# First channel product of batches 5 to 7 and of the tail chunk in seven products instead of eight, in a new searched order

## Chip, cores and metric

One core of one Trainium2 chip runs the kernel. The metric is the device time of one execution in microseconds (us). PE is the matrix engine (TensorE), PEld its weight loads, DVE is VectorE, ACT is ScalarE, POOL is GpSimd, SP is SyncE, which only issues transfers.

## What is computed

Random-feature attention over 8 batches, 8 heads, 576 positions and head size 64 with 128 features, then an MLP-mixer block on its output of width 512:

```python
def phi(x):                                   # x = q or k, scaled by 64 ** -0.25
    h = np.einsum('bhsd,md->bhsm', x, omega) - sum(x * x) / 2.0
    return np.exp(h - max(h)) / np.sqrt(m)
kv = np.einsum('bhsm,bhsd->bhmd', k_p, v)
num = np.einsum('bhsm,bhmd->bhsd', q_p, kv);  den = (q_p . sum over s of k_p) + 1e-06
x = num / den                                 # as [batch, 576, 512]
h = np.maximum(xt @ w_tok1, 0.0) @ w_tok2     # xt: [batch, 512, 576]; w_tok1 576x256
u = x + h.transpose(0, 2, 1)
h2 = np.maximum(u @ w_ch1, 0.0) @ w_ch2       # w_ch1 512x1536, w_ch2 1536x512
out = u + h2
```

## The kernel before

A batch has 512 main positions and 64 tail positions. The tails of all eight batches together make a ninth chunk of 512 positions, called the tail chunk, so the channel MLP runs over nine chunks of 512 positions. Matrix operands are fp16, accumulation is fp32 in eight PSUM banks.

For each batch, `attention` makes the features of k and q (PE, then an exp on ACT), a maximum per position (DVE, L680), its reciprocal (L682), the scaled v (`vs`, a two-input product in SBUF, mostly on POOL, recorded at L295 in the helper `tt`), the product kv (L701), and the numerators (L734, L736), which DVE divides (L743, L744) into the tile `x`. `token_mix` follows (L770, L777, L790), and its sum `u` (L793) is transposed by a DMA (L798) into `uT`.

`channel_mix` takes a chunk of `uT` (for the tail chunk `uTt`). The first channel product (L966) makes twelve blocks of 128 hidden channels; each is four matmuls of 512 columns into one bank, which one relu then moves to the tile `r3` (ACT at L290, or DVE at L292). From chunk 1 on, the second channel product (`channel_out_fast`, L916) already goes by Strassen's scheme in Winograd's form: seven products of 12 matmuls with 256 columns instead of eight, on sums of `r3` blocks that DVE makes in SBUF (tile `S`, L295, two halves of four sums of 128x768) and on weight sums `T` made once. DVE reads its banks to the tile `o` (L905), and SP and ACT store `o`.

All work is cut into jobs. A table of numbers, `ORDER`, sets the order in which the jobs are written out, `SLOT` which buffer or bank each takes, and `MOVED` which engine runs a job that may run on several. Each engine runs its own instructions strictly in that order and waits where an operand is not there. POOL's own queue also issues the loads of q, k and v; loads for later batches are cast to fp16 into DRAM and transposed from there by SP (L380).

Of the rings of buffers, `uT`, `qT`, `kT`, `x`, `u` and `r1` have three buffers each, `qp` and `kp` four, `r3` and `o` two.

Of the kernel before, what the change touches and what calls it, by code (L numbers as in the profile page):

```python
# [9 lines left out]
FP32 = mybir.dt.float32  # L10
# [158 lines left out]
def kernel(  # L169
# [12 lines left out]
    nc = tc.nc  # L182
# [888 lines left out]
```

## Time and profile before

| | |
|---|---|
| device time, median of 3 runs | 277.16 us (276.93 to 277.24) |
| span of the profiled execution | 275.9 us, that is 1.26 below that median; the profile lists no other time of its own for it |
| PE busy | 266.6 us (97%), 2503 matmuls |
| DVE busy | 222.9 us (81%) |
| ACT busy | 138.1 us (50%) |
| POOL busy | 91.2 us (33%) |
| granted PE clock | full in nearly all of the span |

The profile names an instruction by its line, engine and operation and by out<-in tiles. A group's row gives its busy time and the mean length of one instruction in ns; because instructions of one engine overlap a little in their pipeline, the distance from start to start is often shorter than that length. "Idle before" is how long the engine stood still ahead of such instructions, with what ended the wait.

### The profile page before, as it was taken

The page shows a single profiled execution, that of the slowest core. Times are in us where ns is not written, and L with a number is a line of the kernel's source. Part 1 is how long each engine was busy: PE and PEld are TensorE (multiplying, and loading weights), DVE is VectorE, ACT ScalarE, POOL GpSimd, SP SyncE. Part 2 cuts the span into 40 slices and gives each one's busy share as a digit, 9 for nine tenths or more (in the row PEclk, how much of TensorE's full clock was granted, in tenths as well). Part 3 has the DMA queues.
Part 4 walks back from the last instruction along what each step waited for, and adds up shares of the span by engine and source line. Part 5 has one row for each costly group of instructions (what it writes and reads, how often), then busy time and mean ns, then how long its engine had stood idle before and what let it go on. Part 6 is the DMA issues. An engine that isn't in the chain of part 4 may idle for free.

```text
span 275.9 us, 6228 instructions
## 1 busy us (share of the span) xinstructions
PE 266.6 (97%) x2503; PEld 165.5 (60%) x2503; DVE 222.9 (81%) x462; ACT 138.1 (50%) x289; POOL 91.2 (33%) x115
## 2 busy tenths in 40 slices
PE   8789999999999999999999999999999999999993
PEld 3367455444567655755676656755676477446782
DVE  3897889876998799987999899978985992675992
ACT  3999941188685338734756456636654500040200
POOL 8994492063703490075019510600043000000001
PEclk9999999999999999999999999999999999999998
DMA  7999999999998999979989994840252304021125
GB/s 195 192 209 212 190 212 177 202 193 146 203 191 133 229 176 186 151 148 171 198 184 183 232 125 123 191 90 2 97 79 77 96 0 95 2 99 53 78 83 146
DMA packets 81292, 39.66 MB, mean 144 GB/s; under 512 B 63984, under 2 KB 77040, under 8 KB 81072
## 3 DMA queue, kind: packets, MB, share of 16 engines
q0 software_dynamic: 31744, 17.74, 44.2%
q1 hardware_dynamic: 47072, 15.50, 28.7%
q10 hardware_dynamic: 2448, 6.03, 5.6%
q8 instruction: 19, 0.31, 0.5%
q14 instruction: 9, 0.07, 0.1%
HBM read 35.95 MB, written 16.52 MB: 190 GB/s over the span
## 4 chain that ended last, share of the span: by engine, by line
PE 89%; DMA 6%; POOL 3%; DVE 0%; issue 0%; POOLq 0%
PE bank L966 33%; PE bank L916 25%; PE bank L777 5%; PE bank L790 5%; DMA w1m<-in_moe_w_tok_dram 4%; PE bank L1000 4%; PE bank L734 3%; PE bank L656 3%; PE bank L668 2%; PE bank L701 2%; DMA uT<-u 2%; POOL r L319 1%; PE bank L844 1%; PE bank L816 1%; PE bank L828 1%; PE bank L736 1%
## 5 line engine op out<-in xcount | busy, mean ns | idle before, releaser
L966 PE MATMUL bank<-uT,wc 128*128 128x512 f16 x376 | 90.4, 379 | 0.3 <-DMA uT<-u 0.3
L290 ACT ACTIVATE r<-bank 128x512 f16<-128x512 f32 (+1 forms) x84 | 46.9, 597 | 77.1 <-PE bank L966 62.0
L295 POOL TENSOR_TENSOR vs<-v,vs 128x512 f16<-128x512 f16 x31 | 33.2, 1074 | 91.2 <-DVE vs L682 60.5
L966 PEld LDWEIGHTS <-wc 128*128 128x128 f16 x424 | 38.3, 98 | 37.9 <-issue 1.1
L916 PEld LDWEIGHTS <-r 128*128 128x128 f16 x384 | 36.9, 98 | 8.1 <-issue 1.2
L514 ACT ACTIVATE kp<-bank 128x512 f16<-128x512 f32 x64 | 35.6, 622 | 10.4 <-PE bank L656 10.4
L514 ACT ACTIVATE qp<-bank 128x512 f16<-128x512 f32 x64 | 36.3, 616 | 8.9 <-PE bank L668 6.0
L680 DVE TENSOR_REDUCE km<-kp 128x8 f16<-128x1024 f16 x32 | 38.6, 1206 | 2.5 <-ACT kp L514 2.4
L292 DVE TENSOR_SCALAR r<-bank 128x512 f16<-128x512 f32 (+1 forms) x42 | 27.7, 672 | 12.0 <-PE bank L966 11.2
L744 DVE TENSOR_TENSOR x<-bank,rc 128x320 f16<-128x320 f32 x62 | 30.5, 492 | 2.1
L916 PEld LDWEIGHTS <-S 128*128 128x128 f16 x288 | 27.9, 98 | 5.4 <-issue 0.3
L905 DVE TENSOR_TENSOR o<-u,bank 128x512 f32<-128x512 f16 x28 | 19.0, 679 | 6.9 <-PE bank L916 6.8
L916 PE MATMUL bank<-T,r 128*128 128x256 f16 x192 | 23.8, 273 | 0.0
L916 PE MATMUL bank<-T,S 128*128 128x256 f16 x192 | 23.6, 273 | 0.0
L916 PE MATMUL bank<-wc,r 128*128 128x256 f16 x192 | 23.6, 273 | 0.0
L945 POOL DMA_DIRECT2D out_dram<-o x2 | 1.3, 648 | 60.9 <-issue 60.9
L793 DVE TENSOR_TENSOR u<-x,bank 128x512 f16<-128x512 f16 x28 | 17.8, 681 | 1.1 <-PE bank L790 1.0
L905 DVE TENSOR_TENSOR o<-o,bank 128x512 f32<-128x512 f32 (+1 forms) x27 | 16.6, 618 | 2.2 <-PE bank L916 1.6
L734 PEld LDWEIGHTS <-qp 128*128 128x128 f16 x256 | 13.8, 98 | 7.0 <-DVE kvsb L286 0.2
L734 PE MATMUL bank<-kvsb,qp 128*128 128x65 f16 x256 | 15.6, 193 | 0.0
L743 DVE RECIPROCAL rc<-bank 128x5 f32<-128x5 f32 x62 | 11.5, 186 | 4.1 <-PE bank L736 2.7
L701 PEld LDWEIGHTS <-kp 128*128 128x128 f16 x256 | 11.5, 98 | 5.1
(120 smaller groups left out, 376.3 us busy)
## 6 DMA issues: line engine op xcount, KB each, us to landing
out_dram<-o ACTq DMA_DIRECT2D x9, 512.0 KB, 2.6
q<-in_q_dram POOLq DMA_DIRECT2D x6, 576.0 KB, 7.2
wc<-in_moe_w_ch_dram POOLq DMA_DIRECT2D x4, 768.0 KB, 10.6
k<-in_k_dram POOLq DMA_DIRECT2D x6, 512.0 KB, 6.9
v<-in_v_dram POOLq DMA_DIRECT2D x6, 512.0 KB, 8.9
out_dram<-o SPq DMA_DIRECT2D x5, 512.0 KB, 3.9
r<-in_q_dram POOLq DMA_DIRECT2D x4, 288.0 KB, 7.3
v<-in_v_dram POOLq DMA_DIRECT2D x4, 256.0 KB, 8.7
```

Source lines behind the costliest of these rows:

```text
L290: nc.scalar.activation(out=out, in_=in_, func=AF.Relu)
L292: nc.vector.tensor_relu(out=out, in_=in_)
L295: (nc.gpsimd if eng == "POOL" else nc.vector).tensor_tensor(**kw)
L514: nc.scalar.activation(out=out, in_=in_, func=AF.Exp, bias=0.0, scale=1.0)
L680: nc.vector.reduce_max(out=mx, in_=kpv, axis=AX.X)
L701: nc.tensor.matmul(ps[:, i, :], kpv[:, 2 * i + j // 2, j % 2, :], vs[:, i * NJ + j, 0 : D + 1], start=(i == 0 and j == 0), stop=False, ski ...
L734: nc.tensor.matmul(ps[:, k, j * 65 : (j + 1) * 65], st, s[:, i, 0 : D + 1], start=True, stop=True)
L744: nc.vector.tensor_tensor(out=t_x[place("x", b)][:, :, (2 * hp + hs[0]) * D : (2 * hp + hs[0] + n) * D].rearrange("p j (i d) -> p i j d", ...
L793: nc.vector.tensor_tensor(out=t_u[place("u", b)][:, j, :], in0=t_x[place("x", b)][:, j, :], in1=bank(n), op=ALU.add)
L905: nc.vector.tensor_tensor(out=o, in0=a, in1=ps, op=ALU.add)
L916: nc.tensor.matmul(ps[:, j * DH : (j + 1) * DH], a[:, cb, j * P : (j + 1) * P], w[:, cb, :], start=(bank_of(b, j0) not in held and j == j0 ...
L966: nc.tensor.matmul(ps, wc1[:, db, cb * P : (cb + 1) * P], moving(db), start=(db == 0), stop=(db == ND - 1))
```

## The change

From chunk 5 on (`FAST_IN = 5`: chunks 5, 6, 7 and the tail chunk), the first channel product goes by the same seven-product scheme, in `channel_in_fast`. Its 12 blocks of hidden channels are handled in three groups `m` of two blocks from either half. A group's seven products (P1 to P7) have four matmuls of 256 columns each and use three banks, X, Y and Z. P1, P6, P7 and P4 follow each other in bank X: after each of the first three, a copy of the bank in fp32 is kept in SBUF (36 copies in all, on ACT; kept in the upper half of `r3` and in buffers of `qp` and `kp`), since the partial sum is also an addend of another block. DVE then joins a kept copy with a bank (L1097, 36 joins), and the relu of three of the four blocks works on `r3` in place, without a bank. Each chunk needs four sums of `uT` blocks (128x512), and the weights need eight sums of 128x768 once, which live in a `qT` buffer, a `kT` buffer and the new tile `sum`.

Counted over the whole program: 192 matmuls of 512 columns go, 336 of 256 columns come. DVE loses 16 relus from banks, 9 of the divisions at L744 (ACT takes them, 45 more short instructions) and 10 of the 64 sums for `S` (POOL takes them); it gains the 36 joins, 3 relus of banks of the new kind, 9 relus in SBUF and 3 sums of `uT`. ACT loses 32 relus from banks and gains the 36 copies, 9 relus from banks and 15 relus in SBUF. POOL gains 10 sums for `S`, all 8 weight sums and 13 sums of `uT`. PE passes between matmuls of 64 rows and of 128 rows 78 times, 74 before.

Besides, the maximum and its reciprocal are two jobs now, as are the reciprocal and the division of the numerators, so that other work can stand between them; `r1` has two buffers instead of three; the tail chunk's output goes through the buffers of `x`; and the whole of `ORDER`, `SLOT` and `MOVED` is new. `SPLIT` and `HALVES` are empty, so what hangs on them is not built.

```diff
 ORDER = [
-    2, 5, 0, 6, 3, 1, 4, 16, 14, 18, 15, 7, 38, 12, -1, -2, -3, -4, -5, 39, 40, -6, 45, 9, 8, 47, 46, 10, 107,
+    2, 5, 0, 6, 3, 1, 4, 16, 14, 18, 15, 7, 38, 12, -1, -2, -3, -4, -5, 39, 40, -6, 45, 9, 8, 47, 46, 10, 112, 41,
...
+    FAST_IN = 5
+    SPLIT = ()
+    HALVES = ()
...
-             "kvsb": 3, "ktt": 2, "x": 3, "r1": 3, "u": 3, "uT": 3, "r3": 2, "S": 1, "o": 2, "bank": 8}
+             "kvsb": 3, "ktt": 2, "x": 3, "r1": 2, "u": 3, "uT": 3, "r3": 2, "S": 1, "o": 2, "km": 4, "rc": 8, "kmt": 2, "bank": 8}
...
+                nc.vector.reduce_max(out=t_km[place("km", (b, hp))], in_=src_, axis=AX.X)
+            j_m = add("DVE", 0.6, at_["km"], km, deps=j_h, take=[("km", (b, hp))])
+            def km_rec(hp=hp):
                 with nc.allow_low_precision(reason="fp16 operand of the matmul"):
-                    nc.vector.reciprocal(out=vs[:, :, D], in_=mx)
-            j_m = add("DVE", 1.4, at_["km"], km, deps=je, take=[("vs", (b, hp))])
+                    nc.vector.reciprocal(out=t_vs[place("vs", (b, hp))][:, :, D], in_=t_km[place("km", (b, hp))])
+            j_m = add("DVE", 0.15, at_["km"], km_rec, deps=[j_m], take=[("vs", (b, hp))], give=[("km", (b, hp))])
...
+    def weight_sums(key):
+        def quad(i, k, a):
+            return wc1[:, 2 * k + a, i * (DC // 2) : (i + 1) * (DC // 2)]
+        steps = (((1, 0), (1, 1), ALU.add), (0, (0, 0), ALU.subtract), ((0, 0), (1, 0), ALU.subtract), ((0, 1), 1, ALU.subtract))
...
+    def channel_in_fast(c, key, jt):
...
+        steps = ((lambda: block(0, 1), lambda: block(0, 0)), (lambda: block(1, 1), lambda: sums()[:, 0]), (lambda: block(1, 1), lambda: block(0, 1)),
+                 (lambda: block(1, 0), lambda: sums()[:, 1]))
...
+        ops = {
+            "P1": ("X", weights(0, 0), lambda: block(0, 0), []),
+            "P2": ("Y", weights(0, 1), lambda: block(1, 0), []),
+            "P5": ("Z", sum_weights(0), lambda: sums()[:, 0], [j_sums[0][0], j_sums[1][0], j_s[0]]),
+            "P6": ("X", sum_weights(1), lambda: sums()[:, 1], [j_sums[0][1], j_sums[1][1], j_s[1]]),
+            "P7": ("X", sum_weights(2), lambda: sums()[:, 2], [j_sums[0][2], j_sums[1][2], j_s[2]]),
+            "P4": ("X", weights(1, 1), lambda: sums()[:, 3], [j_s[3]]),
+            "P3": ("Z", sum_weights(3), lambda: block(1, 1), [j_sums[0][3], j_sums[1][3]]),
+        }
...
+                    for n in range(2):
+                        for a in range(2):
+                            nc.tensor.matmul(ps[:, n, :], w(a)[:, (2 * m + n) * P : (2 * m + n + 1) * P], x_[:, a],
+                                             start=(what in ("P1", "P2", "P5") and n == 0 and a == 0), stop=False, skip_group_check=True)
...
+            p1 = product("P1", [])
+            p2 = product("P2", [])
+            p5 = product("P5", [])
+            k1 = keep("P1", "X", p1)
+            c11 = join("P1", "Y", 0, 0, [k1, p2], True)
+            p6 = product("P6", [k1])
+            k2 = keep("U2", "X", p6)
+            p7 = product("P7", [k2])
+            k3 = keep("U3", "X", p7)
+            c22 = join("U3", "Z", 1, 1, [k3, p5, c11], False)
+            p3 = product("P3", [c22])
+            c12 = join("U2", "Z", 0, 1, [k2, p3], True)
+            p4 = product("P4", [k3])
...
+        if c >= FAST_IN:
+            channel_out_fast(c, key, channel_in_fast(c, key, jt))
+            return
```

How the order changes is shown at three places of the last stage, which begins when the last batch's `u` is complete.

PE, before: the last two matmuls of the first block of chunk 7 (`uT1`, into bank 1) and the first of its next block (into bank 5). A weight load stands ahead of each matmul, and `wc1` is w_ch1.

```order
L966 MATMUL bank1_64<-uT1_128,wc1_80 128x512
L966 LDWEIGHTS wc1_80
L966 MATMUL bank1_64<-uT1_128,wc1_80 128x512
L966 LDWEIGHTS wc1_80
L966 MATMUL bank5_68<-uT1_128,wc1_80 128x512
L966 LDWEIGHTS wc1_80
```

PE, after: the second half of P6 of group 0 of chunk 7 (into bank 3), and the first half of P6 of group 1 (into bank 5). `uT0` holds the sums of `uT` blocks, `qT0` and `kT1` the weight sums.

```order
L1073 LDWEIGHTS qT0_84
L1073 MATMUL bank3_66<-uT0_126,qT0_84 128x256
L1073 LDWEIGHTS kT1_88
L1073 MATMUL bank3_66<-uT0_126,kT1_88 128x256
L1073 LDWEIGHTS qT0_84
L1073 MATMUL bank5_68<-uT0_126,qT0_84 128x256
L1073 LDWEIGHTS kT1_88
L1073 MATMUL bank5_68<-uT0_126,kT1_88 128x256
```

A product is four matmuls of 256 columns instead of 512, and its bank already holds P1, which ACT must have copied before.

DVE, before: relus from banks of chunk 7 (`r30`) and one of the tail chunk (`r31`), with reads of chunk 6's output `o` among them.

```order
L292 TENSOR_SCALAR r31_131<-bank0_63 128x512
L292 TENSOR_SCALAR r30_130<-bank5_68 128x512
L905 TENSOR_TENSOR o0_132<-u2_126,bank3_66 128x2x256
L292 TENSOR_SCALAR r30_130<-bank0_63 128x512
L905 TENSOR_TENSOR o1_133<-o1_133,bank2_65 128x2x256
L292 TENSOR_SCALAR r30_130<-bank7_70 128x512
L292 TENSOR_SCALAR r30_130<-bank0_63 128x512
L292 TENSOR_SCALAR r30_130<-bank5_68 128x512
L292 TENSOR_SCALAR r30_130<-bank1_64 128x512
L905 TENSOR_TENSOR o1_133<-o1_133,bank4_67 128x2x256
L292 TENSOR_SCALAR r30_130<-bank0_63 128x512
L292 TENSOR_SCALAR r30_130<-bank1_64 128x512
```

DVE, after, at the same place (here `r31` is chunk 7 and `r30` the tail chunk): joins of a bank with a kept copy (`kp`, `qp` or the upper half of `r3`), a relu in SBUF and sums of `uTt` blocks.

```order
L1097 TENSOR_TENSOR r31_130<-r31_130,bank7_70 128x2x256
L1097 TENSOR_TENSOR r31_130<-kp0_99,bank1_64 128x2x256
L312 TENSOR_SCALAR r31_130<-r31_130 128x2x256
L1097 TENSOR_TENSOR r31_130<-kp2_101,bank4_67 128x2x256
L1097 TENSOR_TENSOR r31_130<-qp2_97,bank2_65 128x2x256
L1097 TENSOR_TENSOR r31_130<-qp3_98,bank1_64 128x2x256
L1097 TENSOR_TENSOR r31_130<-qp0_95,bank4_67 128x2x256
L1097 TENSOR_TENSOR r31_130<-kp1_100,bank2_65 128x2x256
L315 TENSOR_TENSOR uT1_127<-uTt_83,uT1_127 128x512
L312 TENSOR_SCALAR r31_130<-r31_130 128x2x256
L1097 TENSOR_TENSOR r30_129<-r30_129,bank1_64 128x2x256
L312 TENSOR_SCALAR r31_130<-r31_130 128x1024 x2
```

Where DVE had one relu per block here, and ACT the rest, it now has three joins per group in a fixed alternation with PE, and further relus behind them.

POOL, before, from the last batch's `vs` to the end: nothing but two stores is left.

```order
L295 TENSOR_TENSOR vs1_104<-v0_90,vs1_104 128x8x64
L295 TENSOR_TENSOR vbd1_114<-vt0_93,vbd1_114 128x8x64
L295 TENSOR_TENSOR vs3_106<-v0_90,vs3_106 128x8x64
L295 TENSOR_TENSOR vs2_105<-v0_90,vs2_105 128x8x64
L295 TENSOR_TENSOR vs0_103<-v0_90,vs0_103 128x8x64
L945 DMA out_0_dram<-o1_133 64x2x256 x2
```

POOL, after: behind the last `vs` stand sums for `S` of chunks 5 and 6 and the sums of `uT` of chunk 7 (`uT2`) and of `uTt`.

```order
L315 TENSOR_TENSOR vs0_103<-v0_90,vs0_103 128x8x64
L315 TENSOR_TENSOR S_71<-r31_130,S_71 128x768
L315 TENSOR_TENSOR S_71<-r30_129 128x768 x2
L315 TENSOR_TENSOR uT0_126<-uT2_128 128x512
L315 TENSOR_TENSOR uT0_126<-uT2_128,uT0_126 128x512
L315 TENSOR_TENSOR S_71<-r30_129,S_71 128x768
L315 TENSOR_TENSOR uT1_127<-uTt_83,uT1_127 128x512
L315 TENSOR_TENSOR uT0_126<-uT2_128 128x512
L315 TENSOR_TENSOR uT0_126<-uT2_128,uT0_126 128x512
L996 DMA out_0_dram<-x2_120 64x2x256 x2
```

POOL's sums moved in ahead of PE's last products, whose operands they are.

More of the change, by code (lines that the diff above doesn't have):

```diff
@@ L104 @@
+    1312: "ACT", 1335: "ACT", 1336: "ACT", 1342: "POOL", 1359: "ACT", 1360: "ACT", 1376: "ACT", 1391: "ACT",
 }
@@ L598, in kt_max @@
                 )
-            j_ktm = add("DVE", 1.2, kkt + 0.01, kt_max, deps=[*j_kte, j_msk], take=[("vbd", b)] if dma_in else [])
+            j_ktm = add("DVE", 0.15, kkt + 0.01, kt_mask, deps=[j_ktm, j_msk], take=take_vbd, give=[("kmt", b)])
             def vbd():
@@ new lines, in rec, with scale @@
+                def rec(hp=hp, i=hs[0], where=where):
+                    nc.vector.reciprocal(out=t_rc[place("rc", (b, hp, i))], in_=where()[:, 0, 0 : 5 * 65].rearrange("p (j d) -> p j d", d=65)[:, :, D])
+                j_r = add("DVE", 0.1, kno, rec, deps=[j_n], take=[("rc", (b, hp, hs[0]))])
+                e_num = engine("DVE")
+                def scale(hp=hp, i=hs[0], where=where, e_num=e_num):
+                    to = t_x[place("x", b)][:, :, (2 * hp + i) * D : (2 * hp + i + 1) * D]
+                    ps = where()[:, 0, 0 : 5 * 65].rearrange("p (j d) -> p j d", d=65)[:, :, 0:D]
+                    rc = t_rc[place("rc", (b, hp, i))]
+                    if e_num == "ACT":
+                        for j in range(NJ + 1):
+                            nc.scalar.activation(out=to[:, j], in_=ps[:, j], func=AF.Copy, scale=rc[:, j : j + 1])
+                    else:
+                        nc.vector.tensor_tensor(out=to, in0=ps, in1=rc.unsqueeze(2).broadcast_to((P, NJ + 1, D)), op=ALU.mult)
@@ L762, in attention @@
+                last_x.append(add(e_num, 0.45, kno, scale, deps=[j_r], take=[("x", b)], give=[at, ("rc", (b, hp, hs[0]))]))
         return last_x
@@ L865, in channel_out_fast @@
             part = slice(g * NH // 2, (g + 1) * NH // 2)
[L866 removed]
+            need = [x for cb in range(part.start, part.stop) for e in range(2) for x in jr[cb + NH * e]]
             steps = (
@@ L944, in store @@
                         to = out[4 * i : 4 * i + 4, SM:S, cols].rearrange("(j h) t d -> h t j d", h=2)[h]
-                        (nc.scalar if eng == "ACT" else nc.sync if eng == "SP" else nc.gpsimd).dma_start(out=to[:, js], in_=t_o[place("o", (c, i))][half[h], js, cols])
-                    dma(eng, key + 0.9, 0.3, store, deps=[outs[need, j] for j in range(*js)], give=[("o", (c, i))],
+                        (nc.scalar if eng == "ACT" else nc.sync if eng == "SP" else nc.gpsimd).dma_start(out=to[:, js], in_=o_of(i)[half[h], js, cols])
+                    dma(eng, key + 0.9, 0.3, store, deps=[outs[need, j] for j in range(*js)], give=[o_tag(i)],
                         cost=0.412 if js[1] - js[0] == 1 else 0.414)
@@ L951, in store @@
             def store(i=i, eng=eng):
-                (nc.scalar if eng == "ACT" else nc.sync).dma_start(out=out[c, 0:SM, :].rearrange("(p j) d -> p j d", j=NJ)[:, 2 * i : 2 * i + 2, :], in_=t_o[place("o", (c, i))])
-            dma(eng, key + 0.9 + 0.1 * i, 1.3, store, deps=[outs[x, 0] for x in need], give=[("o", (c, i))], cost=0.4)
+                (nc.scalar if eng == "ACT" else nc.sync).dma_start(out=out[c, 0:SM, :].rearrange("(p j) d -> p j d", j=NJ)[:, 2 * i : 2 * i + 2, :], in_=o_of(i))
@@ new lines, in channel_out_fast, with sum_of, go @@
+            dma(eng, key + 0.9 + 0.1 * i, 1.3, store, deps=[outs[x, 0] for x in need], give=[o_tag(i)], cost=0.4)
+    j_sums = []
+    def sum_of(i, k):
+        n = 2 * i + k
+        if n < 6:
+            tag = "qT" if n < 3 else "kT"
+            return (t_qT if n < 3 else t_kT)[place(tag, "sums")][:, n % 3 * (DC // 2) : n % 3 * (DC // 2) + DC // 2]
+        return t_sum[:, n - 6]
+    def weight_sums(key):
[3 more added lines that the diff above has]
+        for a in range(2):
+            done = []
+            for i, (x, y, op) in enumerate(steps):
+                e_sum = engine("DVE")
+                def go(i=i, a=a, x=x, y=y, op=op, e_sum=e_sum):
+                    x, y = [sum_of(z, a) if isinstance(z, int) else quad(*z, a) for z in (x, y)]
+                    tt(e_sum, out=sum_of(i, a), in0=x, in1=y, op=op)
+                need = [done[z] for z in (x, y) if isinstance(z, int)]
+                n = 2 * i + a
+                done.append(add(e_sum, 0.46, key, go, deps=[*need, *j_wc1], take=[("qT" if n < 3 else "kT", "sums")] if n < 6 else []))
+            j_sums.append(done)
@@ L1001, in channel_mix @@
                 prev = add("PE", mm(4, 512) + (mm(4, P) if part == 2 else 0.0), key + 0.5 + 0.5 * (3 * j + part) / 12, c2,
-                           deps=[prev, *jr[4 * part : 4 * part + 4], *j_wc2], take=[("bank", n)], give=[("r3", c), ("uT", c)])
+                           deps=[prev, *(x for done in jr[4 * part : 4 * part + 4] for x in done), *j_wc2], take=[("bank", n)], give=[("r3", c), ("uT", c)])
             k2 = key + 0.5 + 0.5 * (3 * j + 3) / 12
```

211 lines of the change are left out of this document (150 added, 61 removed), and 127 rows, old and new, of the table ORDER.

## The prediction

> **What bounds the kernel now.** I read the busy times of the engines first, then stages, then the waits and the chain.
>
> ```profile
> span 275.9 us, 6228 instructions
> PE 266.6 (97%) x2503; PEld 165.5 (60%) x2503; DVE 222.9 (81%) x462; ACT 138.1 (50%) x289; POOL 91.2 (33%) x115
> ```
>
> A modelled busy time of PE may hide gaps, so the stages matter (busy us of PE, PEld, DVE, ACT, POOL, then clock and DMA):
>
> ```profile
> 0.00:30.00 30.00, 25.45 (x379) 15.89 (x380) 21.64 (x54) 24.28 (x59) 22.05 (x35) 1.00 1.11 200
> 30.00:271.00 241.00, 240.71 (x2124) 149.47 (x2122) 200.56 (x408) 113.80 (x231) 69.05 (x80) 1.00 0.75 136
> 224.50:271.00 46.50, 46.50 (x334) 32.49 (x333) 31.99 (x60) 5.92 (x11) 1.15 (x2) 1.00 0.21 66
> 100.00:110.00 10.00, 10.00 (x81) 5.38 (x79) 9.79 (x22) 7.00 (x14) 2.94 (x5) 1.00 1.18 159
> ```
>
> From 30 us to 271 us PE stands still for 0.3 us in all, at full clock; its losses lie in the first 30 us, while operands arrive, and in the last 5. PE's waits say the same; the largest and the only one in a channel product are:
>
> ```profile
> PE bank L1038 <- DVE S L1035: 1.2, 1, 1.2
> ...
> PE bank L966 <- DMA uT<-u: 0.3, 1, 0.3
> ```
>
> The chain in order of time shows the rates (start, length, what):
>
> ```profile
> 234.09 13.81 PE bank L966 x64
> ...
> 260.94 10.51 PE bank L916 x96
> 271.46 0.02 issue
> 271.48 0.42 DVE o L905
> ```
>
> A 512-column matmul thus takes 13.81 / 64 = 0.2158 us and a 256-column one 10.51 / 96 = 0.1095 us. So the kernel is bound by PE's work, and every matmul removed after 30 us shortens it, as long as the others keep pace.
>
> **PE's work.** 192 matmuls of 512 columns go: 192 x 0.2158 = 41.43 us. 336 of 256 columns come: 336 x 0.1095 = 36.79 us. That is -4.64 us, not the -5.2 of one eighth, since a narrow matmul costs more per column. The loads of weights keep up, since L916 runs at 0.1095 with a new load for each matmul as well. A larger price per matmul is the first thing to weigh: the Trainium skill (TensorE: Matmul & The Clock Gate, section Back-to-back issue gap) gives a sustained spacing of about 131 ns for 512 columns and 81 ns for 128; a straight line between them (an estimate) makes 98 ns at 256, and the sum would be 336 x 0.098 - 192 x 0.131 = +7.8 us, about 285 us. Both chain rows speak against that, so I give it no chance.
>
> PE also changes four more times between matmuls of 64 and of 128 rows (78 against 74, all else being counted equal):
>
> ```profile
> 187.83 1.03 PE L966 MATMUL bank<-uT,wc 128*128 128x512 f16 x4
> 188.79 0.40 PE L656 MATMUL bank<-omT,kT 64*128 64x128 f16 x8
> ...
> 194.23 0.38 PE L668 MATMUL bank<-qT,omT 64*128 64x512 f16 x2
> 194.54 1.92 PE L790 MATMUL bank<-r,w 128*128 128x512 f16 x8
> ```
>
> Four matmuls after 187.83 would end at 188.69, but the next starts at 188.79; a pair of 64 rows shares one 0.216, so 194.54 is 0.095 late too. 4 x 0.095 = +0.38 us.
>
> **The others' work in the last stage.** Up to the last `u` there is still attention to put between; from there on only channel products are left, so this stage decides. The rows that price it are groups by shape (busy us, mean ns of one), the view of one line (min/median/max ns) and one row of the timeline:
>
> ```profile
> L290 ACT ACTIVATE r<-bank 128x512 f16<-128x512 f32 x82 | 46.1, 602 | 76.6 <-PE bank L966 62.0 <-PE bank L777 8.9 <-DVE o L905 5.4
> L292 DVE TENSOR_SCALAR r<-bank 128x512 f16<-128x512 f32 x40 | 26.9, 684 | 11.7 <-PE bank L966 11.2
> L295 DVE TENSOR_TENSOR S<-r 128x768 f16<-128x768 f16 x16 | 8.8, 553 | 1.4 <-ACT r L290 1.3
> L905 DVE TENSOR_TENSOR o<-o,bank 128x512 f32<-128x512 f32 x21 | 14.1, 674 | 1.6 <-PE bank L916 1.1 <-issue 0.2
> L905 DVE TENSOR_TENSOR o<-ut,bank 128x256 f32<-128x256 f16 x8 | 3.3, 417 | 0.7 <-PE bank L916 0.7
> L286 ACT COPY o<-bank x2: 586/638/690, 54.7 to 60.1; 128x512 f32<-128x512 f32 x2
> 223.43 1.88 DVE L793 TENSOR_TENSOR u<-x,bank 128x512 f16<-128x512 f16 x3
> ```
>
> By the order, DVE has after the last `u`: 18 joins (no row; the nearest is o<-o,bank, 0.674), 2 relus from banks (0.684), 21 sums (0.553), 14 reads of 512 (0.674) and 14 of 256 (0.417), 3 sums of 512 in SBUF (taken at 0.553) and 6 relus in SBUF. These have no row: not below zero, since it is work, and not above 0.684; I take 0.4. That is 12.1 + 1.4 + 11.6 + 9.4 + 5.8 + 1.7 + 2.4 = 44.4 us, against 32.0 before. PE's stage shrinks by half of 4.64, to 46.50 - 2.32 = 44.2 us. So by lengths DVE would be full. But lengths overlap: three `u` sums take 1.88 us, so (1.88 - 0.68) / 2 = 0.60 from start to start. With 0.08 off each of the 78 instructions it is 38.2 us, 86% of the stage. Before, DVE was 98% busy from 100 to 110 us and PE lost nothing. ACT gets 18 copies (0.638) and 10 relus (0.60 each, three of them of 1024 and taken twice that), 19.3 us of 44, and has room.
>
> **The hand-offs.** In bank X a product must wait for ACT's copy of the one before. The chain shows a reader starting 0.03 us after PE's end, so a hand-off takes about 0.03 + 0.64 plus PE's own start, 0.7 us. By the order the least work that PE has between two such products is 1.3 us (three products of 4 x 0.1095), mostly 1.7 to 3.5. So the cover is there, if ACT is not late with something ahead of the copy in its strict order; at the 1.3 us places one other operation of 0.6 fits and no second. If that cover goes, each operation too many costs 0.6 us of PE. DVE's joins free banks Y and Z in the same way. For the 12 groups the stalls lie between 0 and 12 x 0.6 = 7.2 us; below zero is excluded, as PE had nothing left to gain there. The nearest rows are the 240.71 of 241.00 us and the one wait of 0.3, so I take a value low in it, 0.6 us.
>
> The last `u` still needs its transpose:
>
> ```profile
> DMA to landing us min/median/max: 4.3/5.4/6.0
> ```
>
> After its last token product PE has 68 matmuls of 256 columns in store, 7.4 us, of which DVE's last two `u` sums take 1.3; a transpose of 6.0 us just fits. If DVE comes to those sums later, that is PE's loss one for one. I take 0.1 us.
>
> **POOL and DVE.** POOL has 31 more sums of two operands in SBUF. Only one place of the trace has such an operation on both engines at once:
>
> ```profile
> 14.39 0.60 POOL L630 COPY qpt<-qpt 128x512 f16<-128x512 f16 x1
> 14.52 1.02 DVE L295 TENSOR_TENSOR vs<-v,vs 128x512 f16<-128x512 f16 x1
> 14.96 1.50 POOL L295 TENSOR_TENSOR vs<-v,vs 128x512 f16<-128x512 f16 x1
> ...
> L295 POOL TENSOR_TENSOR vs<-v,vs x31: 1051/1057/1495, 13.4 to 207.9; 128x512 f16<-128x512 f16 x31
> L295 DVE TENSOR_TENSOR S<-r x16: 548/552/559, 74.8 to 261.7; 128x768 f16<-128x768 f16 x16
> ...
> L295 POOL TENSOR_TENSOR T<-vt,T x1: 1941/1941/1941, 34.0 to 34.0; 128x1024 f16<-128x1024 f16 x1
> ```
>
> POOL's `vs` took 1.50 instead of 1.06, as if it stood until DVE's ended at 15.54, so a meeting costs up to 0.5 us. The Trainium skill (SBUF — State Buffer, section SBUF: two separate sides) calls the pair of ports an exclusive lock, held for a whole instruction against a DVE operation with two SBUF inputs; the trace agrees at this one place. DVE's own sums for `S` never took longer than 0.559 us before. A 768 sum on POOL lies between 1.06 and 1.94, half-way 1.5 us. In the last stage POOL has 9 sums (4 of 768, 5 of 512), 11.3 us, mostly at its beginning, where DVE has six sums: six meetings of 0.5 are 3 us of DVE, of which its 6 us of room take most. I take 0.3 us of PE for it.
>
> **Edits that I cost at nothing.** The eight weight sums go to POOL, 8 x 1.5 = 12 us, ahead of the last loads of k and v in its queue. What hides them is POOL's own idle time in those stages (POOL is the fifth pair of numbers):
>
> ```profile
> 160.00:170.00 10.00, 10.00 (x78) 5.71 (x77) 9.74 (x19) 5.18 (x10) 0.43 (x1) 1.00 0.69 111
> ...
> 180.00:190.00 10.00, 10.00 (x90) 5.10 (x89) 8.07 (x22) 4.37 (x9) 0.00 (x0) 1.00 0.30 61
> ```
>
> If that cover is gone, the last loads come late by what is queued ahead, up to 12 us, and PE would wait for batch 7's k by what of it their lead does not take. The 45 more divisions on ACT (L756's kind) and the split of maximum and reciprocal only move DVE work where PE did not wait for DVE at all; they lower DVE's load there. Two buffers of `r1` instead of three put a batch's token relus behind the tail product of the pair before; PE's order has that product ahead. The first 30 us keep their transfers and nearly their order. The end is the same too: a last read of 256, then stores.
>
> **Sum.** 277.16 - 4.64 + 0.38 + 0.6 + 0.1 + 0.3 = 273.9 us. Durations and places are those of the one profiled execution: its span of 275.9 us becomes 275.9 - 3.26 = 272.6, and the 1.26 us between it and the median of the runs stay.
>
> **Rivals.** (1) DVE takes over the last stage. If the lengths do not overlap, DVE needs 44.4 us, and six meetings make it 47.4 against PE's 44.2: 277.16 - 4.26 + 3.2 = 276.1 us. Against it speaks the 0.60 from start to start; for it, that no stretch of 44 us before was as dense (31.99 of 46.5). (2) Slower: the hand-offs in bank X. From 4.26 / 12 = 0.36 us per group on, the gain is gone; if each group has one operation of 0.6 too many on ACT or DVE at one of its tight places, it is 277.16 - 4.26 + 7.2 = 280.1 us. For it: ACT runs in strict order, and in chunks 5 and 6 exps of 0.62 and divisions stand between the copies. Against: PE had no such loss at the many reads of banks in L916. (3) No change: a mixture of both that eats just 4.3 us. That the change does not do what it says is excluded by the counts in the order.
>
> **Chances.** A difference of 0.2%, 0.55 us, is about what a measurement can tell from no change. My forecast's case (272.3 to 275.0) has 0.60, the full DVE (to 276.6) 0.20, no change 0.05, the hand-offs 0.15. Faster is 0.60 + 0.20 = 0.80. The low end has every stall at zero: 277.16 - 4.64 = 272.5, less 0.3 that the new order may win in the first 30 us, 272.2. The high end, 277.0, takes in the full DVE and part of no change, and leaves out the slower case.
>
> **What would show it.** Right: from 30 us on PE at 99% or more, its waits on L1073 under 1.5 us together, L1073 at 0.1095 from start to start, DVE near 86% in the last stage. Wrong: waits of PE for ACT's copies or DVE's joins of several us (rival 2), DVE above 95% in the last stage with PE waiting for it (rival 1), DVE sums of 768 or POOL's sums much longer than 0.553 and 1.5 us (the lock), or gaps ahead of the last chunk for the transpose.

## The result, and the profile after

The changed kernel takes 274.04 us (273.58 to 275.46, four runs) against 277.11 us (276.93 to 277.24): a ratio of 0.990 (0.9877 to 0.9923), 3.07 us less, where 273.9 us had been forecast. In another set of runs it was 274.47 us, ratio 0.9902 (0.9886 to 0.9918). The sum was right; two of its terms were too large and two too small, and the rest of this document takes it apart. In this kernel L1073 are the matmuls of the new products, L961 those of the second channel product, L796 is in `token_mix`, L1097 are the joins, L306 the copies on ACT, L941 the reads of banks, L315 the sums of DVE and POOL, L312 the relus of DVE; in the variants these line numbers are shifted.

The page of the changed kernel, its busy times:

```profile
span 272.0 us, 6648 instructions
PE 262.9 (97%) x2647; PEld 180.0 (66%) x2647; DVE 227.2 (84%) x479; ACT 164.2 (60%) x361; POOL 134.6 (49%) x146
```

Stages of it (busy us of PE, PEld, DVE, ACT, POOL; then clock, share and GB/s of the DMA engines): all from 30 us on, the last stage behind the last `u`, and eleven us out of that stage.

```profile
30.00:267.00 237.00, 236.35 (x2267) 163.46 (x2265) 204.76 (x424) 139.43 (x301) 112.30 (x111) 1.00 0.77 139
222.30:266.75 44.45, 44.20 (x406) 39.33 (x403) 38.74 (x78) 16.14 (x28) 8.54 (x8) 1.00 0.21 68
246.00:257.00 11.00, 11.00 (x103) 9.79 (x102) 10.81 (x21) 5.67 (x9) 0.00 (x0) 1.00 0.01 1
```

PE is as full as before: 236.35 of 237.00 us. The last stage lasts 44.45 us (forecast 44.2) and DVE is busy for 38.74 us of it, 87% (forecast 38.2 and 86%); but from 246 to 257 us it is 98%. PE's waits in this kernel from 30 us on are one row:

```profile
PE bank L1073 <- DMA uT<-u: 0.6, 2, 0.3
```

No wait for a copy, a join or a sum is there: the hand-offs in the banks X and Z and the meetings of POOL and DVE (operations of both in SBUF at the same time) cost PE nothing. The two waits are for transposes, of batches 6 and 7. The chain in order of time shows the second, and the rate of the new products:

```profile
222.46 5.85 DMA uT<-u
...
228.35 1.47 PE bank L1073 x12
...
234.62 10.04 PE bank L1073 x92
...
253.84 13.11 PE bank L961 x120
...
266.98 0.42 DVE x L941
```

92 matmuls of the new products in 10.04 us are 0.1091 us each, 120 of L961 in 13.11 us are 0.1093: the price of the forecast (0.1095), with 0.02 us between PE's end and the last read as before.

To see where the difference lies, I take two fixed places: the first matmuls of `token_mix` behind 47 us, up to which little is changed, and the last six matmuls. The rows of the timeline are those of the kernel before (first profile, then the second one taken below) and of the changed kernel (start, length). A step is the time from one matmul's start to the next one's:

```profile
47.85 0.39 PE L770 MATMUL bank<-x,w1t 64*128 64x512 f16 x2
270.62 0.82 PE L916 MATMUL bank<-wc,S 128*128 128x256 f16 x6
```

```profile
47.57 0.39 PE L770 MATMUL bank<-x,w1t 64*128 64x512 f16 x2
269.88 0.82 PE L916 MATMUL bank<-wc,S 128*128 128x256 f16 x6
```

```profile
47.28 0.39 PE L796 MATMUL bank<-x,w1t 64*128 64x512 f16 x2
266.12 0.82 PE L961 MATMUL bank<-wc,S 128*128 128x256 f16 x6
```

Between the two places lie 222.77 us before (222.31 in the second profile, which lacks the first one's wait for a transpose at 89 us, a step of 0.56 us instead of 0.11), and 218.84 us after: 3.47 us less than in the second profile. PE's work gives -4.64 and the four more switches of rows +0.38. The two waits for transposes are steps of 0.53 and 0.52 us, where 0.03 and 0.11 would be usual, so +0.92. Together -3.34, and 0.13 us are left. Half of them is the price of the new matmuls: at the 0.1093 us of the L961 row PE's work is -4.71, and 0.06 us stay. Behind the last six matmuls the span lasts 275.9 - 270.62 = 5.28 and 275.1 - 269.88 = 5.22 us before, and 272.0 - 266.12 = 5.88 us after: +0.6 us that was not forecast.

### The profile page after: what moved, and what is told of

It reads as the page before. It is cut to its first block, busy times and chain, and to the rows that moved or that the text cites. A ratio compares the mean times of both kernels' runs of the same rounds, so it can differ in the third digit from the quotient of the medians.

```text
span 272.0 us, 6648 instructions
## 1 busy us (share of the span) xinstructions
PE 262.9 (97%) x2647; PEld 180.0 (66%) x2647; DVE 227.2 (84%) x479; ACT 164.2 (60%) x361; POOL 134.6 (49%) x146
## 3 DMA queue, kind: packets, MB, share of 16 engines
q0 software_dynamic: 31744, 17.74, 44.2%
## 4 chain that ended last, share of the span: by engine, by line
PE 86%; DMA 8%; POOL 3%; DVE 1%; issue 0%; POOLq 0%; SPq 0%
PE bank L961 24%; PE bank L1144 19%; PE bank L1073 13%; PE bank L803 5%; PE bank L816 5%; DMA uT<-u 4%; DMA w1m<-in_moe_w_tok_dram 4%; PE bank L1178 4%; PE bank L679 3%; PE bank L768 3%; PE bank L735 3%; PE bank L691 2%; POOL r L339 1%; PE bank L870 1%; PE bank L842 1%; PE bank L854 1%
## 5 line engine op out<-in xcount | busy, mean ns | idle before, releaser
L1144 PE MATMUL bank<-uT,wc 128*128 128x512 f16 x232 | 56.0, 379 | 0.0
L315 POOL TENSOR_TENSOR vs<-v,vs 128x512 f16<-128x512 f16 x31 | 33.1, 1072 | 42.8 <-DVE vs L716 33.5
L310 ACT ACTIVATE r<-bank 128x512 f16<-128x512 f32 (+1 forms) x61 | 34.5, 598 | 26.5 <-PE bank L1144 16.0
L961 PEld LDWEIGHTS <-r 128*128 128x128 f16 x384 | 36.7, 98 | 7.2 <-issue 1.6
L1144 PEld LDWEIGHTS <-wc 128*128 128x128 f16 x232 | 20.5, 98 | 20.1 <-issue 1.1
L961 PEld LDWEIGHTS <-S 128*128 128x128 f16 x288 | 27.7, 98 | 4.7 <-issue 0.4
L786 DVE TENSOR_TENSOR x<-bank,rc 128x320 f16<-128x320 f32 x53 | 25.2, 483 | 1.1
L941 DVE TENSOR_TENSOR o<-u,bank 128x512 f32<-128x512 f16 x28 | 19.1, 680 | 5.8 <-PE bank L961 5.3
L961 PE MATMUL bank<-T,r 128*128 128x256 f16 x192 | 23.8, 273 | 0.0
L961 PE MATMUL bank<-T,S 128*128 128x256 f16 x192 | 23.4, 272 | 0.0
L961 PE MATMUL bank<-wc,r 128*128 128x256 f16 x192 | 23.1, 273 | 0.0
L312 DVE TENSOR_SCALAR r<-bank 128x512 f16<-128x512 f32 (+1 forms) x29 | 18.9, 661 | 3.1 <-PE bank L1144 2.4
L315 POOL TENSOR_TENSOR vbd<-vt,vbd 128x512 f16<-128x512 f16 x6 | 6.4, 1060 | 23.5 <-DVE vbd L616 18.5
L1073 PE MATMUL bank<-uT,wc 128*128 128x256 f16 x120 | 16.6, 273 | 0.6 <-DMA uT<-u 0.6
L941 DVE TENSOR_TENSOR o<-o,bank 128x512 f32<-128x512 f32 x21 | 14.3, 680 | 3.1 <-PE bank L961 2.9
```

What stands on the lines that cost most here:

```text
L310: nc.scalar.activation(out=out, in_=in_, func=AF.Relu)
L312: nc.vector.tensor_relu(out=out, in_=in_)
L315: (nc.gpsimd if eng == "POOL" else nc.vector).tensor_tensor(**kw)
L786: nc.vector.tensor_tensor(out=to, in0=ps, in1=rc.unsqueeze(2).broadcast_to((P, NJ + 1, D)), op=ALU.mult)
L941: nc.vector.tensor_tensor(out=o, in0=a, in1=ps, op=ALU.add)
L961: nc.tensor.matmul(ps[:, j * DH : (j + 1) * DH], a[:, cb, j * P : (j + 1) * P], w[:, cb, :], start=(bank_of(b, j0) not in held and j == j0 ...
```

## Experiments

Ratios are to the kernel before, run beside each variant, with their 95% interval. The changed kernel's own 274.47 us in the first set is the mark for the others. Beside that set the kernel before took 277.08 us, beside the later ones 277.37 to 277.52 us, so a difference to the mark across sets is uncertain by some 0.4 us.

**The same kernel once more.**

> The changed kernel once more, unaltered, as the mark for the others of this round and for a second profile. Theory: the gain is PE's work, 4.64 us less, 0.38 us back for four more switches of rows, 0.4 us less net for waits on transposes; the 0.6 us that PE gained in the first 30 us and the 0.6 us that the end took longer are chance of the one execution. Then the time is 274.0 us (273.5 to 274.6), the last matmul starts 4.0 to 4.7 us after the span's start would put it in the profile before (271.17), that is at 266.5 to 267.2 us, and start and end vary by some tenths. Rival: the new order itself is worth 0.6 us in the first 30 us and costs 0.6 us at the end; then both come again within 0.1 us.

274.47 us. Its two fixed places:

```profile
47.21 0.39 PE L796 MATMUL bank<-x,w1t 64*128 64x512 f16 x2
266.73 0.82 PE L961 MATMUL bank<-wc,S 128*128 128x256 f16 x6
```

The start came out alike, yet that is chance: the variants below have the same order up to there, and their first place lies between 47.0 and 48.0 us, on both sides of the kernel before. The way between the places is 219.52 us, here with a step of 0.79 us instead of 0.11 at 88 us, for a transpose, that the first profile did not have; without it 218.84 again. The end was 272.8 - 266.73 = 6.07 us: the long end belongs to the kernel, as the rival said, though it came again within 0.2 us and not within 0.1.

**Eight products instead of seven.**

```diff
-                    for n in range(2):
+                    for n in (0, 1, 0, 1) if what == "P2" else (0, 1):
```

> The four matmuls of P2 run twice in each of the 12 groups, so that the change has eight products instead of seven, with every sum, copy and join as before; the output is the same. Theory (PE's work sets the time): 48 matmuls more at 0.1095 us are +5.26 us on the changed kernel, 279.3 us, slower than the kernel before by 2.2 us. Rival 1 (DVE is full in the last stage and sets the time there): PE's extra work in the last stage, 24 x 0.1095 = 2.6 us, hides behind DVE, and the time rises by about 2.6 to 3.5 us only, 276.7 to 277.5 us. Rival 2 (a sustained spacing of 98 ns for these matmuls): +4.7 us.

278.86 us, ratio 1.0054 (1.004 to 1.0067): 4.39 us more, not 5.26. The chain has a row of its new products:

```profile
237.90 10.92 PE bank L1073 x100
```

That is 0.1092 us for each, so rival 2 is out, though its 4.7 us lies nearer the result than 5.26: the spacing of 98 ns does not occur. PE has no wait behind 30 us, for `uT` neither: the added matmuls took up the waits for transposes of the unaltered run, 0.37 and 0.52 us by their steps, and 5.26 - 0.89 = 4.37. From the first to the second fixed place it is 270.71 - 47.55 = 223.16 us, 4.32 more than 218.84. So upwards PE's work sets the time whole, at 0.109 us for a matmul, and a full DVE (rival 1) did not hide 2.6 us of it. The gain of the change is the seventh product, and with eight it would be a loss.

**Every kept copy twice.**

```diff
-                    copy(e_keep, kept(what, m), bank(bank_of(b, m)))
+                    for _ in range(2):
+                        copy(e_keep, kept(what, m), bank(bank_of(b, m)))
```

> Each of the 36 kept copies is made twice on ACT, 0.59 us more each; the output is the same. By the trace of the changed kernel the copies end 0.34 us or more ahead of the product that waits for them, six of them less than 0.59. Theory (the hand-offs are covered): PE loses what is missing at those six, 0.2 + 0.15 + 0.1 + 0.07 + 0.07 + 0.06, about 0.7 us, and with the joins that come late after them 0.7 to 2 us, 274.7 to 276.0 us. Rival (the hand-offs set the pace of a group): each group loses 0.6 to 1.8 us, 12 groups 7 to 21 us, 281 us or more.

284.34 us, ratio 1.0239 (1.0214 to 1.0264): +9.9 us, 0.27 us for each of the 36 and 0.8 us for each group. The rival's case came (281 us or more), not the theory's. The stage of chunk 5, in the changed kernel and in this one:

```profile
176.00:192.00 16.00, 16.00 (x176) 11.87 (x174) 14.73 (x33) 14.37 (x32) 9.44 (x9) 1.00 0.35 73
```

```profile
176.00:196.00 20.00, 17.36 (x173) 11.90 (x170) 14.96 (x33) 19.05 (x41) 9.11 (x9) 1.00 0.25 59
```

ACT is busy for 14.37 of 16.00 us there already, and nine more copies of 0.59 us (5.3 us) exceed the 1.6 us that are free: PE stands still for 2.6 us in this window alone. It is the same in the last stage, where ACT has room on average: in the changed kernel it is busy for 6.94 of the 12 us from 234 to 246 us, here for 13.62 of the 14 us from 236 to 250 us, and PE stands still for 2.4 of them. I had counted each copy's own slack as if the copies were apart; ACT does them in one strict row, so a late one makes the next late. The waits of PE show it, spread over many copies:

```profile
PE bank L1073 <- ACT kp L306: 1.8, 4, 0.5
PE bank L1073 <- ACT r L306: 1.6, 5, 0.5
```

**Six products: P3 left out**, so the result lacks it.

```diff
                     ps, x_ = pair(b, m), x()
+                    if what == "P3":
+                        return
```

> The four matmuls of P3 are left out of each of the 12 groups (so the result lacks that product); every copy, join and relu stays. Theory: PE's work is 5.26 us less, 2.63 of it in the last stage, where PE then needs 41.6 us; DVE is busy 38.7 of 44.45 us there, so most is gained, 274.0 - 4.5 = 269.5 us (268.8 to 270.2). Rival (DVE bounds the last stage already): only the half outside the last stage is gained, 274.0 - 2.6 = 271.4 us or more.

273.08 us, ratio 0.9851 (0.983 to 0.9873): 1.4 us gained of PE's 5.26 (its runs lie near 272.4 and near 273.7 us; between the two fixed places of the profile, 47.79 and 264.59 us, it is 2.0 us). The timeline of PE shows new waits, with their length and what ended them at the row's end; the three longest are:

```profile
187.31 0.39 PE L796 MATMUL bank<-x,w1t 64*128 64x512 f16 x2 [0.45 <-DVE x L786]
...
223.13 0.72 PE L961 MATMUL bank<-T,S 128*128 128x256 f16 x5 [0.49 <-DVE S L315]
...
237.95 0.60 PE L1075 MATMUL bank<-uT,kT 128*128 128x256 f16 x4 [0.67 <-ACT qp L306]
```

Downwards PE's work alone no longer sets the time. P3 is also cover: without it PE comes sooner to the next copy, sum or read. Most of these waits stand in the last stage, where the rival put them, but not all, and the longest is for a copy of ACT, not for DVE.

**DVE's sums for S twice.**

```diff
-                    tt(e_sum, out=o[:, part], in0=a[:, part], in1=b[:, part], op=op)
+                    for _ in range(2 if c >= FAST_IN and e_sum == "DVE" and k != 1 else 1):
+                        tt(e_sum, out=o[:, part], in0=a[:, part], in1=b[:, part], op=op)
```

> Of the sums for S of chunks 5 to 8 that DVE makes, those not in place are made twice (19 more, 15 of them behind the last u; at 0.47 us from start to start 8.9 and 7.1 us); the output is the same. Theory A (DVE has as much room in the last stage as it stands idle, 44.45 - 38.74 = 5.7 us): +1.4 to 2.5 us, 275.9 to 277.0 us. Theory B (the idle time lies where it is of no use: DVE is busy 10.81 of 11.00 us from 246 to 257 us, where most of these sums stand): +5 to 7 us, 279.5 to 281.5 us. Theory C (PE alone sets the time): less than +0.5 us.

283.83 us, ratio 1.0233 (1.0207 to 1.0259): +9.4 us for 19 sums that take 8.9 us, more than theory B allowed. Up to 1.3 us of it are two new meetings with POOL's sums of `uT`, in which an operation of DVE took 1.51 instead of 0.55 us (at 201.16 us) and 0.78 instead of 0.42 us (at 230.43 us); the other 8.1 us are still nearly all that the sums take. So the 5.7 us in which DVE stands idle in the last stage were worth next to nothing. The window and the largest waits of PE:

```profile
246.00:277.00 31.00, 25.71 (x225) 21.52 (x222) 29.66 (x61) 7.90 (x14) 1.28 (x2) 1.00 0.13 45
```

```profile
PE bank L962 <- DVE S L315: 3.8, 4, 1.5
PE bank L962 <- DVE x L942: 3.0, 3, 1.4
```

DVE is busy for 29.66 of 31.00 us, and PE for 25.71. So the full DVE (rival 1) did not come to pass, but the changed kernel stands right at its edge.

**Less work for PE in the kernel before.** Six blocks of each of the chunks 5 to 8 leave out a quarter of their product.

```diff
-                for db in range(ND):
-                    nc.tensor.matmul(..., stop=(db == ND - 1))
+                last = ND - 1 if c >= 5 and cb % 2 else ND
+                for db in range(last):
+                    nc.tensor.matmul(..., stop=(db == last - 1))
```

> The kernel before with 24 matmuls of 512 columns less in the first channel product of chunks 5 to 8 (six blocks of each chunk leave out the fourth of their inner size, so the result lacks those terms); nothing else is changed. Theory (PE's work alone sets the time of the kernel before, and what the change gives back lies in its own added work): 24 x 0.2158 = 5.18 us are gained whole, 277.1 - 5.2 = 271.9 us (271.5 to 272.4). Rival (as in the changed kernel without P3, DVE and ACT follow so closely that part is lost): 272.7 to 275 us.

273.91 us, ratio 0.9873 (0.9842 to 0.9905) to 277.37 us: 3.5 us of 5.18. From 175 us on PE waits, where the kernel before had no wait:

```profile
PE bank L916 <- DVE o L905: 0.7, 2, 0.4
PE bank L770 <- DVE x L744: 0.2, 1, 0.2
```

I had read "no wait of PE" as room on the others' side. It is not: the order before was fitted to PE's pace as well, and a third of a saving is lost if nothing else moves. The change kept all of its 4.64 us up to the transposes and the end. That it did so because its order was made anew with it is likely, but not shown: no run has the change in the old order.

**POOL beside DVE.**

```diff
+                    if c >= B - 1 and k >= 2:
+                        beside = t_qT[(place("qT", "sums") + 1) % 3][:, 0 : NH // 2 * 2 * P]
+                        nc.gpsimd.tensor_tensor(out=beside.rearrange("p (n t) -> p n t", n=NH // 2), in0=a[:, part], in1=b[:, part], op=op)
                     tt(e_sum, out=o[:, part], in0=a[:, part], in1=b[:, part], op=op)
```

> POOL makes eight further sums of 128x768, of the same operands as DVE's third and fourth sums for S of chunks 7 and 8, at the same time as those, into a buffer that nobody reads; the output is the same. Theory (lock: where POOL and DVE both work on two operands in SBUF, one stands until the other's instruction ends, whichever holds the port): DVE's sums that meet one become up to 1.6 us longer, and in the full stretch from 246 us on this delays PE by 2 to 8 us, 276 to 282 us. Rival (only POOL gives way, as at 14.96 us in the profiles of before and after): POOL's sums take 2 us or more, DVE's stay at 0.56 us at most, and the time stays within 0.4 us of 274.5.

281.47 us, ratio 1.0145 (1.0122 to 1.0168): +7.0 us, 0.9 us for each of the eight sums. The timeline (start, length) and DVE's sums and relus in SBUF (min/median/max ns), with the changed kernel's rows of the same behind them:

```profile
248.69 1.94 POOL L906 TENSOR_TENSOR qT<-S,r 128x768 f16<-128x768 f16 x1 [1.62 <-DVE S L315]
...
249.05 1.73 DVE L312 TENSOR_SCALAR r<-r 128x512 f16<-128x512 f16 x1
...
250.70 2.45 DVE L315 TENSOR_TENSOR r<-r 128x768 f16<-128x768 f16 x2
250.71 3.94 POOL L906 TENSOR_TENSOR qT<-r,S 128x768 f16<-128x768 f16 x2
...
253.08 0.67 DVE L1100 TENSOR_TENSOR r<-kp,bank 128x512 f16<-128x512 f32 x1
...
L315 DVE TENSOR_TENSOR S<-S,r x16: 549/552/1983, 76.0 to 264.4; 128x768 f16<-128x768 f16 x16
L312 DVE TENSOR_SCALAR r<-r x9: 284/418/1729, 194.1 to 259.9; 128x1024 f16<-128x1024 f16 x5, 128x512 f16<-128x512 f16 x4
```

```profile
L315 DVE TENSOR_TENSOR S<-S,r x16: 549/552/559, 75.3 to 258.5; 128x768 f16<-128x768 f16 x16
L312 DVE TENSOR_SCALAR r<-r x9: 285/418/427, 193.3 to 255.5; 128x1024 f16<-128x1024 f16 x5, 128x512 f16<-128x512 f16 x4
...
L315 POOL TENSOR_TENSOR S<-r,S x6: 1627/1634/1655, 140.5 to 230.7; 128x768 f16<-128x768 f16 x6
```

A DVE sum grew from 0.56 to up to 1.98 us and a relu in SBUF of 128x512, which has one input, from 0.29 to 1.73, while POOL's sums took 1.64 to 2.03: DVE gives way, too. A join of DVE, with one operand in a bank, was not held up (0.67 us at 253.08 us, beside a sum of POOL). So a meeting costs DVE up to 1.4 us, not the 0.5 that I took. The Trainium skill (SBUF — State Buffer, section SBUF: two separate sides) says that whichever of the two starts first holds the shared ports for its whole instruction, against a DVE operation of two SBUF inputs or in a two-port mode; these rows agree.

In the changed kernel the long sums met none: DVE's stay at 0.559 us and POOL's of 128x768 at 1.66 us at most. A short product of DVE did meet one, `vbd`, whose median is 0.19 us. The rows are of the changed kernel, and behind them, of the kernel before:

```profile
157.74 1.64 POOL L315 TENSOR_TENSOR sum<-wc,qT 128x768 f16<-128x768 f16 x1
158.34 1.08 DVE L616 TENSOR_TENSOR vbd<-kmt,mask 128x8 f16<-128x8 f16 x1
```

```profile
118.46 1.06 POOL L295 TENSOR_TENSOR vs<-v,vs 128x512 f16<-128x512 f16 x1 [0.34 <-DVE vs L682]
...
119.10 0.46 DVE L593 TENSOR_TENSOR vbd<-rct,mask 128x8 f16<-128x8 f16 x1
```

Beside a weight sum of POOL it took 1.08 us and ended with that sum; no wait of PE followed. In the kernel before it took 0.46 us and ended with POOL's `vs`. So the prediction's "Only one place" overlooked this one, and here DVE was the one that stood.

**The waits for the transposes.** On DVE, the relu ahead of the last `u` sum of batch 6 goes behind it, and a read of `o` that stood ahead of batch 7's `u` sums goes behind those, with the `u` sum whose product is done last put last (in `ORDER`).

> Two moves on DVE: the relu of chunk 5 that stands ahead of the last u sum of batch 6 goes behind it, and the read of chunk 5's output that stands ahead of the u sums of batch 7 goes behind them, with the u sum whose product is done last put last. Theory (the two waits of PE for uT, 0.43 and 0.41 us beyond the usual step, are the transposes' 6.0 us after the last u sum): both transposes start 0.34 and 0.6 us or more earlier, the waits go, and the time falls by 0.5 to 0.8 us, to 273.7 us by the 274.47 of the same kernel unaltered. Rival (the transpose is late for another reason, or what comes behind waits in its place): no change, 274.2 to 274.7 us.

275.02 us, ratio 0.9921 (0.9894 to 0.9948): no gain. The first wait went, the second grew:

```profile
PE bank L1002 <- DMA uT<-u: 1.3, 1, 1.3
...
221.62 7.52 DMA uT<-u
...
222.19 0.36 ACTq L932 DMA_DIRECT2D out_dram<-o  x1
```

```profile
219.95 0.34 ACTq L1003 DMA_DIRECT2D out_dram<-o  x1
```

The transpose started at 221.62 instead of 222.46 us, and took 7.52 instead of 5.85 us. The read that I moved was the last before a store of 512 KB, which now started 0.57 us behind the transpose (upper rows) instead of 2.5 us ahead of it (the last row is the changed kernel's). That the two slow each other is argued from this; the two kernels below that have the relu's move leave the second one out.

**The end.** The kernel before, for a second profile; then the tail's output through two idle buffers of `qT` instead of `x`; the same with the move of the one relu; and last that move, with `x`, and the halves of the last stores given to SP, ACT and POOL as the kernel before has them.

```diff
-                return t_x[place(*o_tag(i))].rearrange("p j d -> p (j d)")[:, 0 : 4 * DM].bitcast(FP32)...
+                return t_qT[(place("qT", "sums") + 1 + i) % 3][:, 0 : 4 * DM].bitcast(FP32)...
```

```diff
-    939, 942, 1075, 926, 1080, 1233, 1219, 1203, 1220, 925, 1186, 940, 1081, 957, 1077, 1204, 783, 941, 784, 1082,
+    939, 942, 1075, 926, 1080, 1233, 1219, 1203, 1220, 925, 1186, 940, 1081, 1077, 957, 1204, 783, 941, 784, 1082,
```

```diff
-    1438, 1421, 1436, 1428, 1439, 1431, 1422, 1433, 1432, 1440, 1434,
+    1438, 1421, 1436, 1428, 1439, 1432, 1422, 1433, 1431, 1440, 1434,
...
+    1435: "ACT", 1436: "SP", 1437: "ACT", 1438: "SP",
```

> The kernel before, unaltered, for a second profile of it. In the first one its last matmul began at 271.17 us and its span ended 4.7 us after that; the changed kernel and three of its variants showed 4.9 to 5.9 us for that end, and PE reached the first L691 after 31 us between 30.7 and 31.9 us after the span's start. Theory (the end of the changed kernel is slower by its order): the end is 4.7 us again, within 0.15. Rival (chance): it lies anywhere from 4.7 to 5.9 us.

> The output of the tail chunk goes through two idle buffers of qT instead of two buffers of x; all instructions and their order stay. Theory (the end, 4.7 us after the last matmul in both profiles before and 4.9 to 5.9 in the changed kernel and its variants, is longer since stores that read the buffers of x land later): the end falls to 4.7 us and the time by 0.6 us, to 273.9 us by the 274.47 of the unaltered kernel. Rival (the order of the stores, or chance): the end stays at 5.3 us or more and the time at 274.2 to 274.8 us.

> The output of the tail chunk through buffers of qT, and the one relu of chunk 5 moved behind the last u sum of batch 6 (without the second move, which let a store of 512 KB run beside the transposes). Theory: the wait of 0.3 to 0.46 us at 200 us goes as it did with both moves, the one at 228 us stays at 0.4 to 0.5 us, so 0.4 us less than the kernel with the other buffers alone: 273.5 us if the buffers matter, 274.1 us if they don't.

> The relu of chunk 5 behind the last u sum of batch 6 (as in the run with both edits, which gave 274.08 us), the tail's output through x as in the changed kernel, and its stores' halves given to the queues as the kernel before has them: of the first four of the last eight stores, SP's take positions 64 to 127 and ACT's 0 to 63, then the other way round, and POOL stores the upper half first; in the changed kernel SP has the lower half throughout and ACT the upper. Theory (the longer end comes from each queue holding one half of the partitions throughout): the end falls from 5.3 to 5.6 to 4.7 us and the time to 273.5 us. Rival (it comes from elsewhere): the end stays at 5.2 us or more and the time at 273.8 to 274.4 us.

From the last matmul's start on (0.55 us into the last six), the span lasts 4.7 us in both profiles of the kernel before, 5.3 and 5.5 us in those of the changed kernel, and 5.3 us with the buffers of `qT` (274.4 us, 0.9905, 0.9875 to 0.9935), 5.6 us with the relu's move besides (274.08 us, 0.9872, 0.9845 to 0.99) and 5.2 us with the halves exchanged (273.81 us, 0.989, 0.9859 to 0.9922). The stores themselves land later in the changed kernel; SP's and ACT's of the second profile before, of the changed kernel, and of the one with exchanged halves (two stores of 128 KB among each ten, the rest of 64 KB):

```profile
L945 SPq DMA_DIRECT2D out_dram<-o x6: 489/582/798, 266.6 to 271.2; - x6
DMA to landing us min/median/max: 2.4/2.8/3.1
L945 ACTq DMA_DIRECT2D out_dram<-o x4: 545/608/941, 269.2 to 271.6; - x4
DMA to landing us min/median/max: 2.5/2.9/3.4
```

```profile
L996 SPq DMA_DIRECT2D out_dram<-x x5: 493/591/736, 262.7 to 267.5; - x5
DMA to landing us min/median/max: 2.9/3.3/3.9
L996 ACTq DMA_DIRECT2D out_dram<-x x5: 492/522/1066, 262.7 to 267.6; - x5
DMA to landing us min/median/max: 2.6/3.4/4.0
```

```profile
DMA to landing us min/median/max: 2.8/3.2/3.8
DMA to landing us min/median/max: 2.6/3.1/3.6
```

The buffers are not the cause. Exchanged halves shortened the landings a little and the end by 0.1 us, within what the same kernel scatters. The variants of the changed kernel have ends from 4.9 us (every copy twice) to 5.9 us (eight products) with stores of the same sizes. Why stores of the same sizes land some 0.5 us later stays open. The one relu behind `u` does take the first wait for `uT` away (both kernels with it have one such wait, of 0.3 and 0.4 us, instead of two), but their times cannot be told from the changed kernel's: no version is shown to beat it.

## Why the forecast held, step by step

- **PE's work**, -4.64: right. The rates came out (0.1091 to 0.1093), and an eighth product costs its 48 matmuls, less the waits that it covers. The 98 ns that I had estimated from the Trainium skill (TensorE: Matmul & The Clock Gate, section Back-to-back issue gap) are not seen in any run here.
- **Switches of rows**, +0.38: fits the difference between the two fixed places within the 0.06 to 0.13 us that stay; no run varies it by itself.
- **Hand-offs**, +0.6: too large; PE has no wait for a copy or join. That the cover is thin was right, but I gave its price wrongly: "one other operation of 0.6 fits" holds for a single place, and not for all, since ACT is at 90% in chunk 5's stage. That ACT "has room" was read off 19.3 of 44 us, the average of the last stage, and even there copies made twice filled ACT for 14 us.
- **The last transpose**, +0.1: too small. That "a transpose of 6.0 us just fits" named the right risk; DVE came to the last two sums of `u` later, behind a read of `o`, and PE lost 0.41 us as the text said it would, one for one. I did not look at batch 6's transpose, which cost 0.51 us in the same way.
- **POOL and DVE**, +0.3: too large, as the six meetings of the last stage did not take place, and underpriced for one that does: up to 1.4 us of DVE instead of 0.5. That POOL is the one to give way was read off the meeting at 14.96 us; the one at 119.10 us would have shown DVE. A 768 sum on POOL took 1.63 us, half-way had been 1.5.
- **Nothing for the weight sums, the splits, `r1`, the start**: right, no PE wait points to them, though one weight sum held DVE up for 0.9 us. **"The end is the same too"**: wrong by 0.6 us.
- **Rivals.** DVE was 87% busy in the last stage and PE did not wait for it. Still, the rival was nearer than the 86% tells: next to nothing of the remaining 5.7 us could be used. The hand-offs did not come to cost anything, but the point "0.36 us per group" is close as well, since twelve groups with three more copies each lost 0.8 us a group. Overestimates of 0.9 us and underestimates of 1.4 us offset each other in part, so the sum was better than its terms: the mechanism was right, and that the time came within 0.2 us was luck.

## What to carry to other kernels

An engine without a wait tells only that the others keep pace with its present work: 5 us less on PE, all else kept, gave 3.5 us in the kernel before and 1.4 to 2.0 us in the changed one, while 8.9 us more on DVE cost 9.4 us, and 21 us more on ACT 9.9 us, where their averages were 84% and 60%. So price the work that a change shifts to another engine by that engine's busiest ten us, not by its stage, and do not expect the whole saving in an order that was fitted to the old pace. Sum separately what comes after the bound engine's last instruction, and look up every transfer that a faster engine reaches sooner.

## What the hardware showed that was not expected

- A sum on POOL held up DVE's operations in SBUF for most of its length: 1.98 instead of 0.55 us for a sum, 1.73 instead of 0.29 us for a relu in place with a single input, and 1.08 instead of 0.19 us for a product of 128x8. A join with one operand in a bank kept its 0.67 us.
- A transpose of one chunk took 7.52 instead of 5.85 us when a store of 512 KB started 0.57 us behind it; that the store is the reason is argued from one trace.
- Stores of 64 KB at the end landed after 3.5 us instead of 2.9 (medians of the eight in the first profiles after and before), issued at nearly the same spacing; two changes of buffers and queues did not explain it.
